# Storing the result of two MLPs in transfers of 64 rows

## The chip, the cores and the metric

The kernel runs on one core of a Trainium2 chip. The metric is the device time of one execution in microseconds (us). Before the change the median of three runs is 1635.56 us (1634.09 to 1636.39).

The core has a matrix engine (TensorE, in the profile PE, with its weight loads as PEld), three engines for elementwise work (VectorE or DVE, ScalarE or ACT, GpSimd or POOL) and a synchronising engine (SyncE or SP). Transfers between the device memory and the on-chip memory are run by 16 DMA engines; an issuing engine, here SP and after the change ACT too, only starts them from its instruction queue.

## The reference

```python
attn_out = _attn_ref(**attn_kwargs)          # memory attention, 8 batches x 8 heads x 576 tokens x 64
x = np.ascontiguousarray(attn_out.transpose(0, 2, 1, 3)).reshape(B * S, H * D)   # 4608 x 512
x = _moe_ref(x=x, **moe_kwargs)              # h = x @ w_in; (s * relu(h)^2 + b) @ w_out
return _moe2_ref(x=x, **moe2_kwargs)         # h = x @ w_in; relu(h)^2 @ w_out  -> 4608 x 512
```

The inner width of both MLPs is 2048. The result is 4608 rows of 512 float32, 9.4 MB.

## The kernel before

The first half of the program computes the attention and the first MLP, batch by batch, and leaves x in device memory. The second half, the second MLP, starts some 815 us after the beginning. It works in 9 blocks of 512 tokens (`blk`), each in 16 steps over 128 of the 2048 inner columns (`f`). A step multiplies x with a piece of w_in into `hps` (line 650: every float32 product is three products of split parts), takes the square of its positive part on ACT and DVE, and adds its product with a piece of w_out onto four accumulators `oacc` (line 698), one for each 128 tokens (`t` = 0 to 3). In the last step of a block each accumulator is copied to the on-chip memory as soon as its last product is done: t = 0 and 2 by ACT (line 704), t = 1 and 3 by DVE (line 702), into `oo`, 128 partitions of 512 float32.

The tokens stand in another order inside the program than in the result: batch b, then j (0 to 8), then p (0 to 63), where the token's number in its batch is 9 p + j. So 64 rows that follow one another in `oo` (a group, numbered `grp` = 9 b + j) belong to 64 rows of the result that lie 9 rows apart. One accumulator holds two groups, 128 rows. In the kernel before one transfer stores both where they belong to the same batch (line 707): its target has the dimensions 2 x 64 x 512, its source 128 x 512. Where a batch ends between the two groups, two transfers of 64 x 512 store them (line 710). The last block holds the groups 64, 66, 68 and 70 as first groups; modulo 9 these are 1, 3, 5 and 7, so that all its four stores are of the first kind.

All transfers before are issued by SP, in the order of its queue: in a block first the stores of the block before, then the loads of the next block's x (line 520). A store waits for the copy that fills its `oo`. Two `oo` buffers, each for two accumulators, are used again in the next block, so a copy waits for the stores of the block before. After the last store SP waits until all transfers have landed, and the program ends.

Of the kernel before, what the change touches and what calls it, by code (L numbers as in the profile page):

```python
# [20 lines left out]
def memory_attention_then_two_relu2_mlps(  # L21
# [13 lines left out]
):  # L35
    """The float64 weights come as their bits, and are made float32 on the chip.
    Every float32 operand x of the large products is carried as two float32r
    parts, hi = round(x, 12 bits) and lo = x - hi, which is exact; a product is
    hi*hi + hi*lo + lo*hi, accumulated in float32.

    Partition layout of q, k, v, phi: (head parity, p), with token s = 9 p + j;
    tokens run as (b, j, p) from there on, and the last store puts them back.
    """
    nc = tc.nc
# [4 lines left out]
    P = 128  # L49
    J = S // 64                     # 9 tokens a partition  # L50
    NP = H // 2                     # 4 head pairs
    JG = 3                          # j's handled at a time
    NJG = J // JG
    NF = DFF // P                   # 16
    ND = DM // P                    # 4
    NV = DFF // 512                 # 4
    PW = 256                        # columns of a float64 piece
    NB1 = S // 2                    # 288 tokens a block, first MLP
    NB2 = 512                       # second MLP
    NBLK2 = NT // NB2  # L60
    XG = 1152                       # tokens of one scratch tile
    AHEAD = 2                       # steps by which a h precedes its use
    SPILL = 30                      # step from which the weights of the second MLP are made float32
    FOLD = (0, 10, 14)              # steps of the first batch that fold in a next 512 columns of w_in1
    FIRST = 16                      # parts of weights made float32 before the first product
    scale = 1.0 / float(D) ** 0.5

# [1 line left out]
    const = ctx.enter_context(tc.tile_pool(name="const", bufs=1))  # L69
# [13 lines left out]
    b_sb = const.tile([P, 1], F32, name="b_sb")  # L83
    wsum = const.tile([P, ND], F32, name="wsum")    # [d]: b times the sum of w_out1 over f

    narrow_todo, loaded = [], []

    def narrow_later(src, kind, dst):
        """Queues a piece of a float64 weight, as [128, 256] parts."""
        at = lambda a, c: a[:, c:c + PW]  # L90
        for c in range(0, src.shape[1], PW):
            narrow_todo.append((at(src, c), kind, [at(a, c) for a in dst]))
# [8 lines left out]
    def narrow(n=1):  # L101
        """Makes the next n parts float32, behind what else is ready by then. A float64 is sign,
        exponent E (11 bits), 52 bits; the float32 has E - 896 (8 bits) and 23 of the 52. The high
        word taken as a float32 and scaled by 2^-112 is sign, E - 896 (11 bits), 20 bits, and about
        zero where E is no larger than 896; so 3 places to the left, the sign set again, and 3 bits
        more from the low word."""
        for _ in range(n):
# [29 lines left out]

    # ================= phase 1: attention and the first MLP =================
    p1 = ExitStack()
# [8 lines left out]

    w1 = [w1_p.tile([P, NP, 512], F32, name=f"w1_{n}") for n in range(NV)]
    vp = [vp_p.tile([P, 2, 2, 512], F32R, name=f"vp{n}") for n in range(NV)]  # parity, part  # L150
    e_bd = e_p.tile([P, NP, J, 2 * M], F32, name="e")   # block diagonal: rows and columns by parity
    kb = e_p.tile([P, 2, 2, 2, M], F32, name="kb")      # c, parity, pair of c, m
    vmT = e_p.tile([P, 2, 2, M], F32, name="vmT")       # c, pair of c, m

# [12 lines left out]
    def load_kv(b, i):  # L167
        g, c = divmod(i, 2)
        if b == 0 and i > 2:      # w1 is not there yet
            t = w1[2 + i % 2][:, 2 * (i > 4):2 * (i > 4) + 2]  # L170
            t = t.rearrange("p a b -> p (a b)")[:, :4 * JG * D].rearrange("p (i n j d) -> p i n j d", i=2, n=2, j=JG)
        else:
            t = kv_p.tile([P, 2, 2, JG, D], F32, tag="kv", name="kv")
        js = slice(JG * g, JG * g + JG)
        nc.sync.dma_start(t[:, 0], kv_[b][:, 2 * c:2 * c + 2, js])
        nc.sync.dma_start(t[:, 1], vv[b][:, 2 * c:2 * c + 2, js])
        st["kv", b, i] = t
# [7 lines left out]
    def attention(b):  # L185
        """Attention of batch b up to its probabilities, transposed and split. Each yield
        ends a step: what a step does on the tensor engine needs what other engines did in
        the steps before it, and the other way round."""
        ph = st.pop(("ph", b))
# [36 lines left out]
        kvs = ps_m.tile([P, 512], F32, tag="m", name="kvs")  # L226
        kvp = kvs[:, :4 * D].rearrange("p (c i d) -> p c i d", c=2, i=2)     # c, k or v, d
        sump = kvs[:, 4 * D:4 * D + 4].rearrange("p (c o) -> p c o", o=2)
# [29 lines left out]
        yield 1  # L258
        kvn = sm_p.tile([P, 2, 2, 2, D], F32, tag="kvn", name="kvn")   # c, k or v, twice, d
        for c in range(2):  # L260
# [9 lines left out]
        yield 2  # L270
        # columns of kt and vt: c, pair of c, parity, m; rows: (twice, d)
        ktv = kt.rearrange("p c (n h m) -> p c h n m", n=2, h=2)
# [27 lines left out]
        def scores(qT, early=False):  # L300
            sp = psum(early, [P, JG, 2, 2 * M], "sp")   # j, c, (pair of c, m)
            for j in range(JG):
# [43 lines left out]
        if b == 0:  # L346
            # two groups at once; the second is kept where x1 is later
            t = ost.tile([P, ND * NB1], F32, tag="o", name="second")
# [55 lines left out]
    def v_mem(n):  # L404
        """[(pair, m), f] = v_m @ w_in rows of its head, for 512 columns f and each head parity.
        The parities lie in different rows of the array and different banks, side by side."""
        ts = [ps_m.tile([P, 512], F32, tag="m", name="vps") for _ in range(2)]
# [46 lines left out]
    def x1(acc, b, half, f, g, first, store):  # L454
        """acc += w_out1 (tile f) times g; also, in the first block, w_out1 times 1."""
        n = NB1 + 2 if (b, half) == (0, 0) else NB1
# [8 lines left out]
    def x1_store(acc, b, half, part, last):  # L465
        """The evacuation of acc: onto part, if any, and as s acc + wsum on to memory, if it is the last."""
        t0 = b * S + half * NB1
        o = part
# [27 lines left out]

    # what of the second MLP comes in while the first ends
    wi2, xs, early_pools, early_split = [], {}, [], []

    def split_w(dst, src):  # L500
        """dst[:, 0] + dst[:, 1] = src, a [128, 512] piece of a weight."""
        t = wst.tile([P, PW], I64, tag="t", name="wt").bitcast(F32)
        nc.sync.dma_start(t, src)

        def split():
            nc.scalar.copy(dst[:, 0, :], t)
            nc.vector.tensor_tensor(out=dst[:, 1, :], in0=t, in1=dst[:, 0, :], op=ALU.subtract)
        return split
# [36 lines left out]

    # start: batch 0's attention alone, while the weights come in
    load_phi(0)
# [20 lines left out]

    # Attention of the next batch and the weights come between the products of this one.
    # The first batch goes over the weights in two parts, so that they are needed half as fast.  # L570
    steps = [(0, half, f) for fs in (range(NF // 2), range(NF // 2, NF)) for half in range(2) for f in fs]
# [64 lines left out]

    # ================= phase 2: the second MLP =================
    late_p = ctx.enter_context(tc.tile_pool(name="late", bufs=1, side="right"))
# [23 lines left out]
    steps = [(i, f) for i in range(NBLK2) for f in range(NF)]  # L662
    # (loaded one step, split the next) the pieces of wo2, and of wi2's last columns
    pieces = [(wo2[:, f], wo2d[f]) for f in range(NF)]
# [13 lines left out]
    for i in range(-AHEAD, len(steps)):  # L678
# [17 lines left out]
        for t in range(NB2 // P):  # L696
# [3 lines left out]
            if f == NF - 1:  # L700
                if t % 2:
                    nc.vector.tensor_copy(o[t], acc[t])
                else:
                    nc.scalar.copy(o[t], acc[t])
                grp = (blk * NB2 + t * P) // 64
                if grp % J < J - 1:
                    nc.sync.dma_start(outv[grp // J, grp % J:grp % J + 2], o[t])
                else:
                    for z in range(2):
                        nc.sync.dma_start(outv[(grp + z) // J, (grp + z) % J], o[t][64 * z:64 * z + 64])  # L710

# [28 lines left out]
```

## Time and profile before

| | us |
|---|---|
| median of three runs | 1635.56 |
| span of the profiled execution, first to last instruction | 1634.5 |
| TensorE busy | 1575.2 |
| last matmul ends | 1611.5 |
| last copy of an accumulator ends | 1612.2 |
| last data of the last store moves | 1633.2 |

The profile comes from one execution; its own time is known only as its span, 1.06 us below the median of the runs. Times in the rows count from the span's start. In a row of the timeline the first number is the start, the second how long the instruction or the merged group took. A row on SPq is the issue of a transfer, not the moving of its data: when data move is seen in the DMA share of the windows, the mean busy share of the 16 DMA engines.

### The profile page before, as it was taken

What the parts mean: (1) busy time and instruction counts of PE and PEld (TensorE: products, weight loads), DVE (VectorE), ACT (ScalarE), POOL (GpSimd) and SP (SyncE); (2) the same over time, 40 slices, a digit from 0 to 9 for tenths busy, and PEclk for the clock granted to TensorE, in tenths of its full rate; (3) what the DMA queues carried; (4) which work ended last, traced back from release to release, by engine and by line L of the source; (5) the groups of instructions that cost most, each with busy time, mean ns of one, the idle gap of its engine ahead of it and who ended that gap; (6) DMA issues with size and microseconds to landing.
All of it is one profiled execution on the core that took longest, in us unless ns stands there. A gap on an engine that the chain in (4) does not pass through costs nothing.

```text
span 1634.5 us, 25171 instructions
## 1 busy us (share of the span) xinstructions
PE 1575.2 (96%) x10024; PEld 1358.6 (83%) x10024; DVE 714.6 (44%) x1440; ACT 717.7 (44%) x1630; POOL 54.2 (3%) x72
## 2 busy tenths in 40 slices
PE   5799899999999999999999999999999999999994
PEld 3587889989999999989988888888888888888883
DVE  7999796434444443444252223232323222322221
ACT  5787577555556556567552222232323222222221
POOL 2540000000000000000000000000000000000000
PEclk8999999999999999999999999999999999999997
DMA  7666784303021120104030101010100000000000
GB/s 242 205 216 183 244 263 156 105 2 107 26 88 45 60 73 15 40 17 143 21 126 1 52 0 52 1 47 6 44 9 30 23 26 26 1 26 0 26 0 26
DMA packets 120597, 113.31 MB, mean 69 GB/s; under 512 B 44192, under 2 KB 92320, under 8 KB 120480
## 3 DMA queue, kind: packets, MB, share of 16 engines
q1 hardware_dynamic: 120480, 111.70, 22.1%
q8 instruction: 79, 1.29, 0.3%
q14 instruction: 38, 0.31, 0.1%
HBM read 84.41 MB, written 27.26 MB: 68 GB/s over the span
## 4 chain that ended last, share of the span: by engine, by line
PE 86%; DVE 4%; DMA 4%; ACT 2%; issue 1%; SPq 0%; POOL 0%; ACTq 0%; DVEq 0%; POOLq 0%
PE hps L650 24%; PE oacc L698 24%; PE acc L459 21%; PE hps L439 11%; PE vps L413 2%; DMA wt<-in_moe_w_out_dram 1%; PE kvs L238 1%; DMA wt<-in_moe_w_in_dram 1%; PE sp L305 1%; DMA kv<-in_v_dram 1%; DVE wx L125 1%; DVE wx L119 1%; PE qps L290 1%; DVE wx L123 1%; ACT wx L118 1%
## 5 line engine op out<-in xcount | busy, mean ns | idle before, releaser
L459 PE MATMUL acc<-g,wo 128*128 128x288 f32 (+1 forms) x3072 | 471.6, 299 | 4.1 <-DVE g L448 3.0
L459 PEld LDWEIGHTS acc<-g,wo 128*128 128x128 f32 x3072 | 424.2, 189 | 30.5 <-ACT r L446 11.1
L698 PE MATMUL oacc<-wo,g 128*128 128x512 f32 x1728 | 419.6, 392 | 0.0
L698 PEld LDWEIGHTS oacc<-wo,g 128*128 128x128 f32 x1728 | 324.4, 188 | 73.3
L650 PE MATMUL hps<-xh,wi 128*128 128x512 f32 x1152 | 384.2, 394 | 0.0
L656 DVE TENSOR_TENSOR r<-r 128x512 f32<-128x512 f32 x144 | 99.7, 692 | 462.4 <-ACT r L655 462.3
L655 ACT ACTIVATE r<-hps 128x512 f32<-128x512 f32 x144 | 86.0, 597 | 478.9 <-PE hps L650 478.9
L439 PE MATMUL hps<-pt,vp 128*128 128x288 f32 x1536 | 260.1, 300 | 2.5 <-DVE vp L419 0.9
L650 PEld LDWEIGHTS hps<-xh,wi 128*128 128x128 f32 x1152 | 216.2, 188 | 49.5
L439 PEld LDWEIGHTS hps<-pt,vp 128*128 128x128 f32 x1536 | 220.7, 189 | 19.0 <-issue 10.6
L650 PE MATMUL hps<-xl,wi 128*128 128x512 f32 x576 | 225.5, 391 | 0.0
L448 DVE TENSOR_TENSOR g<-r,g 128x288 fp32r<-128x288 f32 x256 | 120.1, 469 | 231.7 <-ACT g L447 230.5
L445 ACT ACTIVATE r<-hps 128x288 f32<-128x288 f32 x256 | 105.0, 410 | 184.3 <-PE hps L439 180.1
L658 DVE TENSOR_TENSOR g<-r,g 128x512 fp32r<-128x512 f32 x144 | 99.7, 692 | 85.3 <-ACT g L657 85.2
L657 ACT CAST g<-r 128x512 fp32r<-128x512 f32 x144 | 89.5, 621 | 95.6 <-DVE r L656 94.5
L650 PEld LDWEIGHTS hps<-xl,wi 128*128 128x128 f32 x576 | 108.0, 188 | 25.1
L446 ACT ACTIVATE r<-r 128x288 f32<-128x288 f32 x256 | 113.6, 444 | 6.0
L447 ACT CAST g<-r 128x288 fp32r<-128x288 f32 x256 | 110.5, 432 | 6.9 <-PE acc L459 0.4
L118 ACT ACTIVATE wx<-wt 128x256 f32<-128x256 f32 x128 | 55.3, 437 | 33.4 <-DMA wt<-in_moe_w_in_dram 18.5
L413 PE MATMUL vps<-w,vmT 64*32 64x512 f32 x512 | 50.8, 608 | 7.5 <-POOL w L128 5.4
L125 DVE SCALAR_TENSOR_TENSOR wx<-wt,wx 128x256 int32<-128x256 int32 x128 | 57.5, 465 | 0.6
L419 DVE TENSOR_TENSOR vp<-vps,vp 128x512 fp32r<-128x512 f32 x64 | 42.1, 685 | 14.1 <-ACT vp L418 13.2
(222 smaller groups left out, 812.7 us busy)
## 6 DMA issues: line engine op xcount, KB each, us to landing
wt<-in_moe_w_in_dram SPq DMA_DIRECT2D x64, 256.0 KB
wt<-in_moe_w_out_dram SPq DMA_DIRECT2D x64, 256.0 KB
q<-in_q_dram SPq DMA_DIRECT2D x72, 128.0 KB
x1d<-xo SPq DMA_DIRECT2D x16, 576.0 KB
kv<-in_k_dram SPq DMA_DIRECT2D x45, 192.0 KB
kv<-in_v_dram SPq DMA_DIRECT2D x45, 192.0 KB
out_dram<-oo SPq DMA_DIRECT2D x32, 256.0 KB
x<-x1d SPq DMA_DIRECT2D x6, 1024.0 KB
```

What stands on the lines that cost most here:

```text
L439: nc.tensor.matmul(hps[:, :NB1], lhsT=w[:, wi], rhs=pt[xi][:, hp, t0:t0 + NB1], start=(i == 0), stop=(i == 5))
L445: nc.scalar.activation(r[:, :NB1], hps[:, :NB1], AF.Relu)
L446: nc.scalar.activation(r[:, :NB1], r[:, :NB1], AF.Square)
L447: nc.scalar.copy(g[0][:, :NB1], r[:, :NB1])
L448: nc.vector.tensor_tensor(out=g[1][:, :NB1], in0=r[:, :NB1], in1=g[0][:, :NB1], op=ALU.subtract)
L459: nc.tensor.matmul(acc[d][:, :n], lhsT=wo1[:, f, wi, d * P:d * P + P], rhs=g[xi][:, :n], start=(first and i == 0), stop=(store is not None ...
L650: nc.tensor.matmul(hps[:, :NB2], lhsT=w[:, wi], rhs=xs[i][xi][:, d], start=(n == 0), stop=(n == 3 * ND - 1))
L655: nc.scalar.activation(r, hps[:, :NB2], AF.Relu)
L656: nc.vector.tensor_tensor(out=r, in0=r, in1=r, op=ALU.mult)
L657: nc.scalar.copy(g[0], r)
L658: nc.vector.tensor_tensor(out=g[1], in0=r, in1=g[0], op=ALU.subtract)
L698: nc.tensor.matmul(acc[t], lhsT=g[xi][:, t * P:t * P + P], rhs=wo2[:, f, wi], start=(f == 0 and n == 0), stop=(f == NF - 1 and n == 2))
```

## The change

Every accumulator is stored by two transfers of 64 rows, whatever its groups. In the last block (`blk` 8) the second of the two is issued by ACT in place of SP. The rest of the diff takes out comments and is left out here.

```
@@ -702,12 +702,12 @@
-                grp = (blk * NB2 + t * P) // 64
-                if grp % J < J - 1:
-                    nc.sync.dma_start(outv[grp // J, grp % J:grp % J + 2], o[t])
-                else:
-                    for z in range(2):
-                        nc.sync.dma_start(outv[(grp + z) // J, (grp + z) % J], o[t][64 * z:64 * z + 64])
+                for z in range(2):
+                    grp = (blk * NB2 + t * P) // 64 + z
+                    eng = nc.scalar if (z and blk == NBLK2 - 1) else nc.sync
+                    eng.dma_start(outv[grp // J, grp % J], o[t][64 * z:64 * z + 64])
```

The order on PE, DVE and POOL stays as it was. On SP, in the second MLP, the stores stand between the loads of x for the blocks that follow; the piece begins with the last load of a weight and ends with the program:

```order
 L503 DMA wt<-wo2d_98 128x512
 L520 DMA x<-x1d_76 128x4x512
-L707 DMA out_dram<-oo 2x64x512 x4
+L709 DMA out_dram<-oo 64x512 x8
 L520 DMA x<-x1d_76 128x4x256
 L520 DMA x<-x1d_77 128x4x256
-L710 DMA out_dram<-oo 64x512 x2
-L707 DMA out_dram<-oo 2x64x512 x3
+L709 DMA out_dram<-oo 64x512 x8
 L520 DMA x<-x1d_77 128x4x512
```

Each block's stores stay at their place between the same loads; there are eight in place of four or five, and four in the last block.

On ACT the end of the program before was this (in brackets what an instruction waits for; oo_14996 holds t = 0 and 1 of the last block, oo_14997 t = 2 and 3):

```order
L655 ACTIVATE r_15407<-hps_15394 128x512 [waits PE_49,Activation_49]
L657 CAST g0_15408<-r_15407 128x512 [waits DVE_49]
L704 COPY oo_14996<-oacc_14992 128x512 [waits DMAHW6_49,DMAHW5_49,PE_49]
L704 COPY oo_14997<-oacc_14994 128x512 [waits DMAHW1_49,DMAHW7_49,DMAHW0_49,PE_49]
L735 UNCONDITIONAL_BRANCH
```

And it is this after the change (oo_15024 and oo_15025 are the same two buffers):

```order
L655 ACTIVATE r_15435<-hps_15422 128x512 [waits PE_49,Activation_49]
L657 CAST g0_15436<-r_15435 128x512 [waits DVE_49]
L704 COPY oo_15024<-oacc_15020 128x512 [waits DMAHW6_49,DMAHW1_49,DMAHW7_49,DMAHW0_49,PE_49]
L709 DMA out_0_dram<-oo_15024 64x512 [waits Activation_49]
L704 COPY oo_15025<-oacc_15022 128x512 [waits DMAHW4_49,DMAHW3_49,DMAHW5_49,DMAHW2_49,PE_49]
L709 DMA out_0_dram<-oo_15024 64x512 [waits DVE_49]
L709 DMA out_0_dram<-oo_15025 64x512 [waits Activation_49]
L709 DMA out_0_dram<-oo_15025 64x512 [waits DVE_49]
L735 UNCONDITIONAL_BRANCH
```

ACT now issues the store of the upper half of t = 0 between its two copies, and those of t = 1, 2 and 3 behind the second copy.

## Rows read from the trace of the kernel before

**Rows 1.** The page, busy time of each engine and its share of the span.

```profile
PE 1575.2 (96%) x10024; PEld 1358.6 (83%) x10024; DVE 714.6 (44%) x1440; ACT 717.7 (44%) x1630; POOL 54.2 (3%) x72
```

**Rows 2.** The chain that ended last, from 1600 us: start, us, what.

```profile
1603.28 8.21 PE oacc L698 x36
...
1611.51 0.69 DVE oo L702
```

**Rows 3.** Windows: us, engines' busy us (instructions), clock, DMA share, GB/s; the program's end.

```profile
1611.20:1611.30 0.10, 0.10 (x2) 0.00 (x0) 0.00 (x0) 0.10 (x1) 0.00 (x0) 1.00 0.10 41
...
1614.00:1630.00 16.00, 0.00 (x0) 0.00 (x0) 0.00 (x0) 0.00 (x0) 0.00 (x0) 0.52 0.13 50
...
1633.10:1633.20 0.10, 0.00 (x0) 0.00 (x0) 0.00 (x0) 0.00 (x0) 0.00 (x0) 0.50 0.10 41
1633.20:1633.30 0.10, 0.00 (x0) 0.00 (x0) 0.00 (x0) 0.00 (x0) 0.00 (x0) 0.50 0.01 0
1633.30:1634.50 1.20, 0.00 (x0) 0.00 (x0) 0.00 (x0) 0.00 (x0) 0.00 (x0) 0.50 0.00 0
```

**Rows 4.** What SP's queue waited for, from 1600 us: us, times, longest.

```profile
SPq L735 <- DMA out_dram<-oo: 13.5, 3, 5.1
```

**Rows 5.** Timeline of the last block's copies and stores: start, us, engine, line.

```profile
1609.47 0.59 ACT L704 COPY oo<-oacc 128x512 f32<-128x512 f32 x1 [4.12 <-PE oacc L698]
1610.08 9.86 SPq L707 DMA_DIRECT2D out_dram<-oo  x4
1610.15 0.69 DVE L702 COPY oo<-oacc 128x512 f32<-128x512 f32 x1 [4.08 <-PE oacc L698]
1610.83 0.59 ACT L704 COPY oo<-oacc 128x512 f32<-128x512 f32 x1 [0.77 <-PE oacc L698]
1611.51 0.69 DVE L702 COPY oo<-oacc 128x512 f32<-128x512 f32 x1 [0.67 <-PE oacc L698]
```

**Rows 6.** Timeline of SP's queue, a pair of 64-row stores in block 1.

```profile
995.91 1.18 SPq L710 DMA_DIRECT2D out_dram<-oo  x2
```

**Rows 7.** Windows around that pair.

```profile
997.10:997.20 0.10, 0.10 (x2) 0.05 (x2) 0.10 (x1) 0.10 (x1) 0.00 (x0) 1.00 0.77 205
997.20:997.40 0.20, 0.20 (x3) 0.16 (x2) 0.20 (x2) 0.06 (x1) 0.00 (x0) 1.00 0.95 215
...
998.50:998.60 0.10, 0.10 (x2) 0.06 (x1) 0.00 (x0) 0.00 (x0) 0.00 (x0) 1.00 0.41 41
998.60:998.70 0.10, 0.10 (x2) 0.10 (x1) 0.00 (x0) 0.00 (x0) 0.00 (x0) 1.00 0.00 0
```

**Rows 8.** Windows of a load of x, 128 partitions, 1 MB.

```profile
902.00:903.00 1.00, 1.00 (x6) 0.84 (x5) 0.36 (x1) 0.60 (x1) 0.00 (x0) 1.00 0.91 324
903.00:904.00 1.00, 1.00 (x6) 0.83 (x5) 0.33 (x1) 0.00 (x0) 0.00 (x0) 1.00 1.04 401
```

**Rows 9.** Lines 707 and 710: ns of an issue (min/median/max), first and last start.

```profile
L707 SPq DMA_DIRECT2D out_dram<-oo x32: 511/546/4961, 907.4 to 1615.0; - x32
```

**Rows 10.** SP's queue from 907 us, stores and the next loads of x.

```profile
907.38 10.18 SPq L707 DMA_DIRECT2D out_dram<-oo  x4
988.00 1.27 SPq L520 DMA_DIRECT2D x<-x1d  x2
```

**Rows 11.** Windows of two whole blocks, columns as in rows 3.

```profile
907.00:995.00 88.00, 88.00 (x383) 71.63 (x382) 25.61 (x38) 22.14 (x38) 0.00 (x0) 1.00 0.07 24
1438.00:1526.00 88.00, 88.00 (x383) 71.67 (x382) 23.49 (x34) 20.18 (x34) 0.00 (x0) 1.00 0.04 13
```

**Rows 12.** The program's first transfer on SP's queue.

```profile
0.74 0.45 SPq L164 DMA_DIRECT2D ph<-in_phi_dram  x1
```

**Rows 13.** Windows of the program's start.

```profile
1.00:1.50 0.50, 0.00 (x0) 0.00 (x0) 0.00 (x0) 0.50 (x1) 0.50 (x1) 1.00 0.00 0
1.50:2.00 0.50, 0.00 (x0) 0.00 (x0) 0.00 (x0) 0.50 (x1) 0.50 (x1) 1.00 0.21 53
```

## The prediction

> **What bounds the kernel now.** The page comes first: PE is busy for 1575.2 us of a span of 1634.5, so almost all of the time is matmul work that this change doesn't touch [rows 1]. The chain that ended last says what follows it: it closes with 36 matmuls of line 698 up to 1611.5 us and the copy of the last accumulator by DVE up to 1611.51 + 0.69 = 1612.20 [rows 2]. The chain stops there, yet the span goes on for another 22.3 us. The reader should ask at once what ends the program, and the waits of SP's queue answer it: 13.5 us of waiting, in three waits, for stores of `oo` [rows 4]. The windows of the end show how these stores move: in 1614 to 1630 the DMA share is 0.13 and the rate 50 GB/s, with no engine at work [rows 3]. 0.13 of 16 engines are two engines (2/16 = 0.125). The first data move in 1611.2 to 1611.3, the last end in 1633.2 to 1633.3: the four stores of the last block, 4 x 256 KB = 1.05 MB, take 22 us, that is 48 GB/s, and then 1634.5 - 1633.2 = 1.3 us pass to the end of the program [rows 3]. So the last 21 us are bound by two DMA engines, 14 others idle.
>
> In the body the same slow stores cost nothing. In a whole block PE is busy for 88.00 of 88.00 us, with stores in it at this low rate [rows 11]. SP's queue issues a block's stores within 10.18 us and then waits until 988 us to load the next x, for a buffer and not for the stores [rows 10].
>
> **The change part by part.** *The shape of a store.* The trace has 64-row stores already, where a batch ends inside an accumulator. A pair of them was issued at 995.91 in 1.18 us, 0.59 each [rows 6]; its data move from the window 997.10 to 997.20 until that of 998.50 to 998.60, at a share of 0.77 to 0.95 and 205 to 215 GB/s in its first part [rows 7]. So these stores run on all engines. From the start of an issue to its data pass 997.13 - 995.91 = 1.2 us (997.13 for a window that is busy at 0.77), the same as for the first store of the end, 1611.27 - 1610.08 = 1.19 [rows 3, 5]. The two take about 1.45 us, 0.72 each, for 128 KB: 181 GB/s against 48.
>
> A rule speaks against pieces of 64 rows. [Rows 7, 8] show it in the trace: a 64-row store reaches 205 to 215 GB/s, a load to 128 partitions 324 to 401, both at a share above 0.9. The Trainium skill, page "SBUF — State Buffer", section "Door 1: The DMA port swizzle", has it that partitions 0 to 63 reach only 8 of the 16 ports on the DMA side, and 64 to 127 the other 8. By that rule the two halves of an accumulator moved at once would not hinder each other, which is the sum below; the trace before never moves both halves at once, so that no run here shows that part. The page "DMA: Bandwidth & Descriptors", section "Issuing engines are not separate DMA queues", says that a second issuing engine saves only issue time; by it the second queue would give no rate of its own, which is the first rival.
>
> *The issues of the end.* SP's stores wait for the copies, which don't move: 1609.47 + 0.59 = 1610.06 (t = 0), 1610.15 + 0.69 = 1610.84 (t = 1), 1610.83 + 0.59 = 1611.42 (t = 2), 1612.20 (t = 3) [rows 5]. SP issues the lower half of each right behind, at 1610.08, 1610.85, 1611.44 and 1612.21, and none waits for the one before (0.59 < 0.59 + 0.02 at the closest). ACT issues the upper halves. No row shows an issue on ACT; SP's are between 0.51 and 4.96 us, the long ones while two engines are still full of earlier stores [rows 9, 10]. I take the 0.59 of the 64-row pair, the nearest. Then ACT is busy with the upper half of t = 0 from 1610.07 to 1610.66; behind it in ACT's queue waits only the copy of t = 2, which cannot start before its matmul anyway, at 1610.83: 0.17 us of cover, so this insertion costs nothing, and at an issue of 1.0 us 0.24 us. After the copy, from 1611.43, three issues: at 1611.43, 1612.02 and 1612.61 (t = 3, its copy done since 1612.20).
>
> *The end.* The last data start at 1612.61 + 1.2 = 1613.81, move for 0.72, and end at 1614.5; with the 1.3 us from the last data to the end of the program the span is 1615.8. For the first use of ACT's queue I add nothing: SP's first transfer was issued at 0.74 and its data move from within 1.50 to 2.00, at most 1.26 us later, no more than in the middle of the program [rows 12, 13]. From below: an ACT issue of 0.51 [rows 9] and data at the 401 GB/s of [rows 8], 0.33 us for 128 KB, give 0.16 + 0.39 = 0.55 less, 1615.3. From above: four issues on ACT of 4.96 us each, worked out among the rivals.
>
> *The body.* Eight issues a block in place of four or five: 8 x 0.59 = 4.7 us, with 70 us of waiting behind them in the same queue [rows 10]; nothing. Their 1 MB comes in bursts at some 200 GB/s in place of 20 us at 50. Beside the burst of [rows 7] PE is busy for 0.10 of 0.10 and 0.20 of 0.20 us, beside the load of [rows 8] for 1.00 of 1.00; nothing. A gain isn't there either, since nobody waits for these stores.
>
> *The sum.* 1634.5 - 1615.8 = 18.7 us less in the profiled execution. The median of the runs is 1635.56, 1.06 above that execution's span; I keep that distance: 1615.8 + 1.06 = 1616.9, written as 1617.0, 1.1% faster.
>
> **The rivals.** *First: the halves share one rate.* All eight stores together move no faster than the pair of [rows 7]: from 1611.27, 8 x 0.72 = 5.8 us, until 1617.0; span 1618.3, time 1619.4. For it: 64-row stores are the only ones on 16 engines that the trace has, and their rate is half of the load's. Against it: the load shows that the engines can do 401 GB/s, and the halves are different partitions.
>
> *Second: issuing on ACT stalls as it did on SP.* SP needed 9.86 us for four issues at the end [rows 5]. With 4.96 us for each of ACT's: the first until 1615.03, the copy of t = 2 until 1615.6, then three, the last starting at 1625.5; its data end at 1627.4, span 1628.7, time 1629.8. Against it: the stalls stand behind stores that fill two engines, and 64-row stores leave no such backlog; the pair went at 0.59 each.
>
> *Third: the stores stay slow.* If at the end the device memory or the two kinds of queue, not the number of engines, set the rate of 50 GB/s, the change doesn't do what it says, and the time stays 1635.6. Against it: the rate in the pair's windows.
>
> *Fourth, slower: the second queue has a price of its own around the program.* Before, one queue issues every transfer, and 1.06 us lie between the span and the median. If preparing ACT's queue, once for each execution and ahead of the first instruction, costs more than the 18.7 us that are saved, the kernel is slower; with 25 us it would be 1616.9 + 25 = 1642. It decides from 18.7 us on. For it: no row has such a queue, so nothing in the trace excludes it. Against it: the queue of SP began to move data 1.26 us after its first issue, and all that lies around the span with it is 1.06 us.
>
> **How the numbers follow.** A measurement of this kernel can't tell less than about 0.2%, 3.3 us, from no change. The forecast (1617.0, with its bounds 1616.4 to 1618) has 0.66, the shared rate 0.22, the stall on ACT 0.06, the stores that stay slow 0.03, the price of the second queue 0.03. The first three are faster by more than 0.2% (1629.8 by 0.35%): 0.94; the fourth is the same, 0.03; the last is slower, 0.03. The range takes in the forecast and the shared rate, 0.88 of the chance, from 1616.4 to 1619.4, each widened by the 1.2 us or so that runs of the kernel before differ from their median: 1615.0 to 1620.6.
>
> **What would show it right or wrong.** In the profile after, the DMA share of the windows behind 1611.3 should be well above 0.13, and the data should end near 1614.5; near 1617 it is the shared rate, at 200 GB/s throughout. The DMA section should list a second queue with about 0.5 MB. ACT's issues should take about 0.6 us, and its copy of t = 2 should start at 1610.83 as before. The last matmul should still end at 1611.5; if it has moved by more than a microsecond, the body is not as indifferent as I take it to be. The wait of SP's queue for the stores should shrink from 13.5 us to 2 or 3. A span that falls by 18 us while the time doesn't would be the fourth rival, and data at 50 GB/s the third.

## The result, and the profile after

The changed kernel takes 1618.57 us (median of four runs, 1616.92 to 1620.07); its ratio to the kernel before is 0.9884, 95% interval 0.9869 to 0.9900 (the quotient of the two medians, 0.9896, lies inside it). The prediction was 1617.0, range 1615.0 to 1620.6. The profile after is of the slowest of the four executions, 1620.07 us with a span of 1618.3.

First the end of the chain that ended last, against [rows 2]: start, us, what.

```profile
1605.09 8.21 PE oacc L698 x36
...
1613.32 0.69 DVE oo L702
```

The last matmuls end at 1613.3, 1.8 us later than before; the last copy starts at 1613.32, and 5.0 us later the span ends, against 23.0 before (1634.5 - 1611.51). This *tail*, from the start of the last copy of an accumulator to the end of the span, is what the change touches; it is the measure of all that follows, since the work ahead of it shifts from run to run by more than a microsecond.

The timelines of the last block's stores, SP's queue and ACT's, against [rows 5]:

```profile
1611.89 2.61 SPq L709 DMA_DIRECT2D out_dram<-oo  x4
```

```profile
1611.28 0.59 ACT L704 COPY oo<-oacc 128x512 f32<-128x512 f32 x1 [4.12 <-PE oacc L698]
1611.90 0.56 ACTq L709 DMA_DIRECT2D out_dram<-oo  x1
1612.65 0.59 ACT L704 COPY oo<-oacc 128x512 f32<-128x512 f32 x1 [0.78 <-PE oacc L698]
1612.68 0.60 ACTq L709 DMA_DIRECT2D out_dram<-oo  x1
1613.33 0.75 ACTq L709 DMA_DIRECT2D out_dram<-oo  x1
1614.41 0.47 ACTq L709 DMA_DIRECT2D out_dram<-oo  x1
```

ACT's first issue (0.56 us) fits ahead of its second copy, which starts 1.37 us behind the first, as before (1610.83 - 1609.47 = 1.36). Its second issue stands behind that copy in the order, yet starts at 1612.68, while the copy runs until 1613.24: the issue doesn't wait for the end of the copy ahead of it. The copy that fills its own buffer, DVE's of t = 1, ends at 1612.65. The last one starts at 1614.41, 0.40 us after the copy it waits for; why not sooner, no row says.

The windows of the end, against [rows 3]; the last columns are the granted clock, the DMA share and GB/s:

```profile
1613.00:1613.50 0.50, 0.28 (x2) 0.00 (x0) 0.18 (x1) 0.23 (x1) 0.00 (x0) 1.00 0.89 197
1613.50:1614.00 0.50, 0.00 (x0) 0.00 (x0) 0.50 (x1) 0.00 (x0) 0.00 (x0) 1.00 0.99 328
1614.00:1616.50 2.50, 0.00 (x0) 0.00 (x0) 0.01 (x1) 0.00 (x0) 0.00 (x0) 1.00 0.93 310
...
1616.70:1616.90 0.20, 0.00 (x0) 0.00 (x0) 0.00 (x0) 0.00 (x0) 0.00 (x0) 1.00 0.06 21
1616.90:1618.30 1.40, 0.00 (x0) 0.00 (x0) 0.00 (x0) 0.00 (x0) 0.00 (x0) 1.00 0.00 0
```

The share is about 0.9 and more in place of 0.13, the rate 310 GB/s in place of 50, and the eight stores take 3.8 us (1613.0 to some 1616.85), where the four took 22. SP's last wait shrinks from 13.5 us [rows 4] to 2.4:

```profile
SPq L735 <- DMA out_dram<-oo: 2.4, 1, 2.4
```

Where do the 1.8 us of a later last matmul come from? Not from the second MLP: the copies of ACT run from 908.6 to 1612.6, 704.0 us, as from 906.8 to 1610.8 before, also 704.0. They lie ahead of it, where the change moves nothing. A delay is there early: the square of the first MLP (ACT, line 445) that starts at 54.99 us in the profile before starts at 56.96 in the one after, 2.0 us later. In both profiles the granted clock is 0.50, the lower level of 1.2 GHz, all through 30 to 40 us, with PE busy for 7.8 of the 10. In the next 10 us its mean is 0.95 before and 0.67 after, so that it is back at 2.4 GHz later, and seven matmuls of line 439 take 2.05 us in place of 1.19. But this delay is not simply what is left at the end: the square that starts at 362.57 before starts at 362.99 after, only 0.4 us later, and 1.8 us are there again at the first copy. What brings them is not shown. The repetitions below show that such a shift comes and goes with the same program.

### The profile page after: what moved, and what is told of

The parts are those of the page before. It is cut to its first block, busy times and chain, and to the rows that moved or that the text cites. A ratio compares the mean times of both kernels' runs of the same rounds, so it can differ in the third digit from the quotient of the medians.

```text
span 1618.3 us, 25231 instructions
## 1 busy us (share of the span) xinstructions
PE 1579.7 (98%) x10024; PEld 1363.8 (84%) x10024; DVE 714.8 (44%) x1440; ACT 717.7 (44%) x1630; POOL 54.2 (3%) x72
## 3 DMA queue, kind: packets, MB, share of 16 engines
q1 hardware_dynamic: 121120, 111.18, 23.2%
## 4 chain that ended last, share of the span: by engine, by line
PE 87%; DMA 4%; DVE 4%; ACT 2%; issue 1%; SPq 1%; POOL 0%; ACTq 0%; DVEq 0%; POOLq 0%
PE hps L650 25%; PE oacc L698 25%; PE acc L459 21%; PE hps L439 11%; PE vps L413 2%; DMA wt<-in_moe_w_out_dram 2%; DMA wt<-in_moe_w_in_dram 1%; PE kvs L238 1%; DMA kv<-in_v_dram 1%; PE sp L305 1%; DVE wx L125 1%; PE qps L290 1%; DVE wx L123 1%; DVE wx L119 1%; ACT wx L118 1%
```

## The experiments

Runs that were taken together share a chip and the runs of the kernel before to which their ratios refer. The edits are to the changed kernel.

**One queue.** 64-row stores everywhere, all from SP:

```
-                    eng = nc.scalar if (z and blk == NBLK2 - 1) else nc.sync
+                    eng = nc.sync
```

Expected: 

> Only the shape changes: 64-row stores everywhere, all issued by SP, in the last block too. Measured as the tail, from the end of the last matmul to the end of the span (before: 23.0 us, after the change: 5.0 us), since the part ahead of it moves by up to 2 us from run to run. Theory (the number of DMA engines that a store's shape gives it is what counted, the second queue only saves issue time): eight issues on one queue at 0.63 us (the pace of a block's eight stores in the profile after, 5.03 us), the last starts 8 x 0.63 - 0.63 = 4.4 us after the first, 3.0 us after the last matmul, then 1.2 to the data, 0.65 of data, 1.6 to the end: a tail of 6.5 us, time 1.5 us above the changed kernel, some 1620. Rival (the second queue gave most of it): a tail of 15 to 23 us, time 1628 to 1636.

Measured: 1619.04 us, ratio 0.9895 (0.9874 to 0.9915). The tail is 1616.0 - 1609.64 = 6.4 us; chain, SP's queue and the data of this run:

```profile
1609.64 0.69 DVE oo L702
```

```profile
1608.22 4.96 SPq L709 DMA_DIRECT2D out_dram<-oo  x8
```

```profile
1610.00:1614.00 4.00, 0.00 (x0) 0.00 (x0) 0.34 (x1) 0.00 (x0) 0.00 (x0) 1.00 0.88 205
```

The shape alone gives 23.0 - 6.4 = 16.6 of the 18.0 us; the rival falls. One queue moves the data at 205 GB/s, two at 310. Its eight issues come 4.96 / 8 = 0.62 us apart, the last at 1612.6, 3.0 us after the start of the last copy; with two queues the last one starts 1.1 us after it.

**Two queues, old shape.** The 2 x 64 x 512 stores as before, in the last block t = 1 and 3 from ACT:

```
+                if grp % J < J - 1:
+                    (nc.scalar if (t % 2 and blk == NBLK2 - 1) else nc.sync).dma_start(
+                        outv[grp // J, grp % J:grp % J + 2], o[t])
...
```

Expected: 

> Only the second queue: the stores of 2 x 64 x 512 as before the change, in the last block t = 0 and 2 from SP, t = 1 and 3 from ACT. Theory (both queues feed the same two engines): data at 50 GB/s as before, a tail of 23 us, time as before, 1636. Rival (the rate belongs to a queue, or each queue gets engines of its own): twice the rate, a tail of some 13 us, time 1626.

Measured: 1637.93 us, ratio 1.0009 (0.9997 to 1.0020), a tail of 1638.2 - 1615.11 = 23.1 us. Its windows while the stores move:

```profile
1616.00:1636.00 20.00, 0.00 (x0) 0.00 (x0) 0.00 (x0) 0.00 (x0) 0.00 (x0) 0.58 0.13 49
```

Still 0.13 and 49 GB/s: both queues together get no more than two engines' worth, as the theory has it, and the rival's doubled rate is out. The second queue without the shape is worth nothing; it also has no measurable price in the time.

**Last block only, and all but the last block.** In the first, only the last block has 64-row stores from two queues, in the second only the eight blocks ahead of it:

```
+                if blk < NBLK2 - 1 and grp % J < J - 1:       # first;  second: blk == NBLK2 - 1 and ...
+                    nc.sync.dma_start(outv[grp // J, grp % J:grp % J + 2], o[t])
...
```

Expected of the first: 

> 64-row stores and the second queue in the last block only; the eight blocks ahead store as before the change. Theory (the body gains nothing): a tail of 5.0 us and the time of the changed kernel, 1618.6 within 1.5 us. Rival (slow stores in the body cost PE something, or the many stores of the change cost something there): the stretch from the first to the last copy of an accumulator on ACT, 704.0 us in both profiles, differs by more than 0.5 us.

Expected of the second: 

> 64-row stores in the eight blocks ahead of the last, the last block stored as before the change, from SP alone. Theory (all of the gain is at the end): a tail of 23 us and the time of the kernel before, 1636 within 1.5 us. Rival (part of the gain comes from the body): 1 us or more below the kernel before with the tail at 23 us.

Measured: the first 1620.05 us, ratio 0.9896 (0.9873 to 0.9919), a tail of 1614.0 - 1609.37 = 4.6 us; the second 1637.99 us, ratio 1.0007 (0.9994 to 1.0020), a tail of 1634.7 - 1611.47 = 23.2 us. The second is 2 us above the 1636 that was expected, but the kernel before beside it is at 1636.76, so that the ratio decides. The copies on ACT in the first, and in the second:

```profile
L704 ACT COPY oo<-oacc x18: 587/587/587, 904.6 to 1608.7; 128x512 f32<-128x512 f32 x18
```

```profile
L704 ACT COPY oo<-oacc x18: 587/587/588, 906.7 to 1610.8; 128x512 f32<-128x512 f32 x18
```

Both run over 704.1 us: the shape of the stores in the body neither costs nor gains. All of the gain is in the last block. The end of the first is that of the changed kernel, and its tail is 4.6 where that has 5.0: single profiles of one end differ by some tenths of a microsecond.

**Four phases of stores.** Behind the end of the changed kernel, 2 MB of extra stores to a scratch tensor in each of four phases:

```
+    for n in range(8):      # A (B: ACT also src[(n + 1) % 4][0:64];  C: both from nc.sync)
+        nc.sync.dma_start(scr[2 * n], src[n % 4][0:64])
+        nc.scalar.dma_start(scr[2 * n + 1], src[n % 4][64:128])
...
+    for n in range(8):      # D
+        nc.sync.dma_start(scf[128 * n:128 * n + 128], src[n % 4])
```

Expected: 

> The changed kernel with four phases of extra stores to a scratch tensor behind its end, 2 MB each, 16 stores of 64 rows (A, B, C) or 8 of 128 rows (D), each phase held apart by a load of the scratch; its whole time says nothing. A: SP stores lower halves (partitions 0 to 63), ACT upper halves. B: both store lower halves. C: SP alone, lower and upper in turn. D: SP alone, 128 partitions in one store, target contiguous. Theory (a 64-row store is limited by the half of the partitions that it reads, and two queues are faster since they move both halves at once): A 300 to 400 GB/s, B 180 to 220, C 200 to 220 (one store is nearly done before the next begins), D 350 to 400. Rival (the second queue itself gives the rate, by more transfers at once, whatever the halves): A and B alike, both at 300 or more.

Measured in one execution, one window inside each phase, A to D:

```profile
1622.00:1627.00 5.00, 0.00 (x0) 0.00 (x0) 0.00 (x0) 0.00 (x0) 0.00 (x0) 0.50 0.96 312
1634.00:1641.00 7.00, 0.00 (x0) 0.00 (x0) 0.00 (x0) 0.00 (x0) 0.00 (x0) 0.50 0.97 208
1648.00:1656.00 8.00, 0.00 (x0) 0.00 (x0) 0.00 (x0) 0.00 (x0) 0.00 (x0) 0.50 0.87 203
1662.00:1666.00 4.00, 0.00 (x0) 0.00 (x0) 0.00 (x0) 0.00 (x0) 0.00 (x0) 0.50 1.06 407
```

The issues of B's eight stores on SP, and of one of C's:

```profile
1631.19 7.38 SPq L727 DMA_DIRECT2D scr<-oo  x8
...
1646.87 0.60 SPq L731 DMA_DIRECT2D scr<-oo  x1
```

Two queues with the same half of the partitions (B) stay at 208 GB/s with all engines busy; with different halves (A) they reach 312; one queue with all 128 partitions (D) reaches 407. In B stores queue up: eight issues on SP take 7.38 us, where they took 5.56 in A, and a store lands up to 5.0 us after its issue. So it is the half of the partitions that limits the stores there, and a second queue alone brings no rate.

C, one queue with the halves in turn, is no faster than B, but for another reason. Its issues come 0.64 us apart (1646.87, 1647.51 and so on), about as long as B's 208 GB/s need for 128 KB, 0.63 us, and each of its stores lands 2.2 to 2.4 us after its issue, so that nothing queues up: by these numbers one half is nearly done before the other begins. The same holds for the end of the kernel with one queue, 0.62 us apart and landing after 2.2 to 2.4 us. So the second queue helps by issuing sooner, which brings two stores under way at once, and this gives a rate only where they read different halves. Whether one queue that issued faster would reach A's 312 GB/s too is not tested.

The Trainium skill, page "SBUF — State Buffer", section "Door 1: The DMA port swizzle", gives some 218 GB/s as the rate that transfers of partitions 0 to 63 approach; B's 208 agrees with it. That the two halves at once would not hinder each other, as the prediction worked out from that section, the runs show only in part: 312 GB/s are 1.5 times 208, not twice. The Trainium skill, page "DMA: Bandwidth & Descriptors", section "Issuing engines are not separate DMA queues", has it that a second issuing engine saves only issue time. The runs agree: in B and with the old shape the second queue brings no rate, and at the end of the kernel it lets the last issue start 1.9 us sooner (1.1 us after the start of the last copy against 3.0).

**A spread end.** The last two steps of the last block run accumulator by accumulator, and the last copy is shared by ACT and DVE:

```
+        if blk == NBLK2 - 1 and f == NF - 2:
+            continue
+        todo = [(f, gs.pop(i))]
+        if blk == NBLK2 - 1 and f == NF - 1:
+            todo.insert(0, (f - 1, gs.pop(i - 1)))
         for t in range(NB2 // P):
+            for ff, g in todo:
...
+                if blk == NBLK2 - 1 and t == NB2 // P - 1:
+                    nc.scalar.copy(o[t][:, :DM // 2], acc[t][:, :DM // 2])
+                    nc.vector.tensor_copy(o[t][:, DM // 2:], acc[t][:, DM // 2:])
```

Expected: 

> The changed kernel with a shorter end: in the last block the last two steps of 128 inner columns run accumulator by accumulator, so that the accumulators are ready 1.37 us apart and not 0.68, and the last one is copied by ACT and DVE, half of the columns each. Theory: with the stores of t = 0 to 2 out of the way the last two stores take 0.35 (copy) + 1.2 + 0.5 + 1.6: a tail of 3.7 us in place of 5.0, time 1.3 us below the changed kernel, about the bound of what can be measured. Rival (the end is bound by the landing of each store, not by the stores queued up): a tail above 4.5 us.

Measured: 1617.95 us, ratio 0.9888 (0.9871 to 0.9904), beside 0.9897 (0.9882 to 0.9912) of the changed kernel taken with it; the difference lies within the intervals. The chain's end in this run:

```profile
1613.92 0.38 ACT oo L707
...
1614.32 0.42 DVE oo L708
```

The tail is 1618.4 - 1613.92 = 4.5 us (4.65 from the end of the last matmul at 1613.75), neither 3.7 nor clearly the rival's, and hardly below the 4.6 of the last block alone, so that no gain is shown. The two halves of the copy ran one after the other (DVE waits for ACT's half), 0.82 us in place of the 0.35 that was expected; that is 0.47 of the 0.8 us missing. The rest is the data of the last two stores, which move from some 1615.9 to 1617.0, 1.0 to 1.1 us where 0.5 was counted, with 1.4 us behind them where 1.6 was.

**The changed kernel again.** Twice, unedited, once taken with the spread end and once with the last experiment. Expected: 

> The changed kernel once more, beside the others of this call. Every theory: a tail of 5.0 us, ratio to the kernel before 0.988 to 0.990; its last matmul ends at another time than in the profile at hand (1613.3) by up to 2 us, since that 1.8 us more than in the profile before is a difference of the program's first 49 us, not of the stores.

And: 

> The changed kernel beside it: a tail of 5.0 to 5.2 us, as in its two profiles so far.

Measured: 1619.44 us, ratio 0.9897 (0.9882 to 0.9912), a tail of 1617.7 - 1612.49 = 5.2 us; and 1618.42 us, ratio 0.9895 (0.9879 to 0.9912), a tail of 1617.4 - 1612.46 = 4.9 us. The second tail is just below the 5.0 to 5.2 that were expected. The last copies start at 1612.49 and 1612.46 in place of 1613.32: the work ahead of the end does shift between runs of one program. That it is the first 49 us that decide, as was expected, doesn't follow: in 40 to 50 us the mean granted clock is 0.51 and 0.50 here, lower than the 0.67 of the profile with the latest end.

**128-row stores.** In the last block x is split in another order of its columns, so that the partitions of an accumulator are pairs of neighbouring rows of the result, and one store takes all 128:

```
+                if i == NBLK2 - 1:
+                    vs = lambda a: a.rearrange("k (t j p) -> k t j p", j=2, p=64)
+                    vd = lambda a: a.rearrange("k (t p j) -> k t j p", j=2, p=64)
...
+    outp = out.rearrange("(b p j) d -> b p j d", b=B, j=J)
...
+                if blk == NBLK2 - 1:
+                    nc.sync.dma_start(outp[grp // J, :, grp % J:grp % J + 2], o[t])
...
```

Expected: 

> The other way to all engines: in the last block the split of x (lines 525 and 526 of before) writes the columns of each 128 tokens in the order (p, j) in place of (j, p), so that the 128 partitions of an accumulator are pairs of neighbouring rows of the result, and one store per accumulator has the target dimensions 64 x 2 x 512, which lie as 64 runs of 4 KB; all four from SP, no second queue; 64-row stores from SP in the other blocks. Theory (what counts is how many engines, and which partitions, a store takes at once): four stores at some 400 GB/s, 0.65 us each, issued as the copies end, 0.68 us apart, so that nothing queues up: last copy 0.7 after the last matmul, then 1.2, 0.65 and 1.6: a tail of 4.2 us against 5.0 to 5.2 of the changed kernel and 6.4 of 64-row stores from SP alone. Time 0.8 us below the changed kernel, which is within what can be measured. Rival (a second queue is needed to get below 6 us, or a store whose target has two dimensions ahead of the row runs on fewer engines): a tail of 6 us or more; if a store got two engines again, 23 us.

Measured: 1616.02 us, ratio 0.9885 (0.9870 to 0.9899), and the changed kernel beside it 0.9895. The chain's end and the data of this run:

```profile
1609.39 0.69 DVE oo L708
```

```profile
1610.00:1610.50 0.50, 0.00 (x0) 0.00 (x0) 0.08 (x1) 0.00 (x0) 0.00 (x0) 1.00 1.02 401
```

A tail of 1613.5 - 1609.39 = 4.1 us, 0.8 to 1.1 shorter than in the three profiles of the changed kernel (0.5 shorter than in the last block alone), with one queue and four issues. The tail is as expected, and all engines move the data (a share of 1.02 at 401 GB/s), though the target has two dimensions ahead of the row: 64 x 2 in place of 2 x 64. In the times the advantage over the changed kernel lies within the intervals.

## Why the prediction was right

*The place and the cause.* The prediction put all of the gain into the last block and onto the number of engines that a store takes. The last block alone gives it (tail 4.6), the rest of the program nothing (tail 23.2, ratio 1.0007), the shape without the second queue 16.6 us of it, the queue without the shape nothing. A store of all 128 rows whose target starts with 64 in place of 2 gives it with one queue (4.1).

*The size.* 18.7 us were predicted for the tail, 4.3 in place of 23.0; it is 5.0 in the profile after, a gain of 18.0. The step that is mis-sized is the data of the last store. It was counted with 0.72 us behind its issue, as if nothing were queued ahead of it; the last data should have ended 2.3 us after the last copy (1614.5 - 1612.2). They end in the window up to 1616.9, 2.7 to 2.9 us after the last copy's end at 1614.01. The eight stores move at 310 GB/s, which is A's 312, not at the load's 401 that spoke for the choice, and so the last one waits for its turn: the halves do hinder each other, if less than by a shared rate. (That the trace before never moves both halves at once holds for its 64-row stores alone; the load to 128 partitions does.) The shared rate, the first rival, would have needed 5.8 us for the eight, the forecast some 3.3; they took 3.8, so the truth lies nearer to the forecast. The time alone would not have told: the median, 1618.57, is nearer to the rival's 1619.4 than to 1617.0, and that the span of the profile after is the rival's 1618.3 is chance, as its end is 1.8 us late. The issues on ACT take 0.47 to 0.75 us, near the 0.59 that was taken, so the second rival falls, and with 310 GB/s the third. That they would queue up behind ACT's second copy was wrong (the second starts during it), but the last one starts 1.09 us after the start of the last copy (1614.41 - 1613.32), where 1612.61 - 1611.51 = 1.10 was predicted. That this fits is luck: it was to wait for the issues ahead of it, and in fact it starts 0.40 us after its own copy for a reason that no row shows.

*The distance from span to time.* 1.06 us were added to the span, the difference between one execution's span and the median of other executions. That was the wrong pair: where a run's own time and span are both known they differ by 1.77 us (1620.07 - 1618.3), and by 1.74 with SP's queue alone (1617.74 - 1616.0, one queue). The profile before would then be of an execution of about 1636.3, above its median. The same difference answers the fourth rival: it is 1.74 to 1.83 us in the later runs of the kernel before and 1.97 to 2.08 with two queues and the old shape, so that a second queue adds at most some 0.3 us around the span, not 18. The tail (0.7), the distance (0.7) and the late end of the last matmul (1.8) together lead from 1616.9 to the 1620.1 of the profiled execution.

*The range.* By its own working its lower end is 1616.4 - 1.2 = 1615.2, not 1615.0, and the upper bound of the forecast, 1618, is worked out nowhere; the result hangs on neither.

*The body.* Nothing was the right cost there, by the copies' 704.0 to 704.1 us in every variant that leaves the order of the matmuls alone. That the last matmul would still end at 1611.5 was not right: it moved by 1.8 us, ahead of the first copy. The prediction had named such a shift as a sign that the body is not indifferent; the copies show that it isn't one, since single profiles of kernels with the same first half have their last copy anywhere from 1609.37 (last block only) to 1615.11 (two queues, old shape).

## What to carry to other kernels

Look at what the program waits for after its last computation, and read the DMA share of that stretch as a number of engines: 0.13 of 16 are two, and a store whose target starts with a dimension of 2 was given two. Here the shapes that start with 64 were worth 16.6 to 18.9 of the 23.0 us of that stretch, and nothing in the body, where nobody waits for the transfers. For an effect at one end of the program compare that end in the profiles (23.0, 6.4, 5.0, 4.1 us), not whole times that differ by 2 us between executions.

## What the runs showed that was not expected

Stores from the two halves of the partitions on two queues add up to 312 GB/s, not to the 407 of stores from 128 partitions, though all engines are busy in both (0.96 and 1.06); why, no run shows. ACT issues a transfer while the copy ahead of it in the order still runs (1612.68 us, the copy from 1612.65 to 1613.24). And the same program reaches its last copy anywhere between 1612.46 and 1613.32 us, for a reason that stays open.
